# Attention times values on 128 partitions: one bank per pair of heads, copied behind the exponentials, and chunks of 55 columns

## The chip, the cores and the metric

The kernel runs on one core of a Trainium2 chip. The metric is the device time of one execution in microseconds (us); each time given is the median of three runs, and the profile is of one further execution.

## The reference

The reference is an attention with heads that are mixed before and after the softmax, followed by a gated feed-forward layer:

```python
batch, n_heads, seq, head_dim = (4, 12, 448, 64)          # B, H, S, D
scores = scale * np.matmul(q, k.transpose(0, 1, 3, 2))
scores = np.einsum('bhij,hg->bgij', scores, w_pre)
scores = scores - np.max(scores, axis=-1, keepdims=True)
attn = np.exp(scores)
attn = attn / (np.sum(attn, axis=-1, keepdims=True) + 1e-09)
attn = np.einsum('bhij,hg->bgij', attn, w_post)
x = np.matmul(attn, v)                    # then reshaped to 1792 x 768
xn = x / sqrt(mean(x * x) + 1e-06) * rms_g
out = (silu(xn @ w_gate) * (xn @ w_val)) @ w_out           # 768 -> 1536 -> 768
```

All inputs and outputs are float32.

## The kernel before

The program has two parts. Part A is the attention, up to about 360 us; part B is the feed-forward layer, and the change doesn't touch its code.

Part A cuts the 448 queries of each of the four batches into `NC` = 4 chunks of 120, 120, 120 and 100 columns (`OFF`, `PAIRS`), of which the last 12 are padding. A chunk is worked through in steps: `PAIRS` = 6, 6, 6, 5 steps, 92 in all (`T`). A step is called a pair (n, p): chunk n, pair p. Each step has two halves `u`, and each of them two groups `v_` of `RH` = 5 queries with all 12 heads, so that 60 rows of a 64-row tile are used.

The order of the instructions is written out by hand (`manual_schedule`, the loop over `t` at line 470). In step t TensorE issues, in this order:

- `premix` of step t (tile `sp`, line 186) in turn with `qk_mm` of a later chunk (tile `qk`, line 138). Both use tiles of 64 rows by 64 columns of the array.
- `postmix` of step t-1 (tile `pm`, line 227): 28 small products of 60 by 64, 60 columns each, which write the mixed attention transposed.
- `av_mm` (tile `av`, line 271): the product with v for a block of two chunks that are done, one half (`part` 0 or 1) of a pair of heads in each step. The stored attention `at_all` has keys on the partitions, in two halves `m` of 64; the two halves are multiplied by themselves in 64 by 64 tiles, and go to two PSUM banks `o[0]` and `o[1]`.

ScalarE (ACT) then does `av_copy` of both banks, if a pair of `av` was finished in the step before, and after it the exponentials `expo` (line 200), its half of the evacuation of `qk` (line 160, tile `st`) and its half of the evacuation of `pm` (line 242, `evac_a`). VectorE (DVE) takes the row maxima (line 193) and the other halves. GpSimd (POOL) adds the two copies of `av` (line 294, through `sum_ops`), squares and sums them (lines 301 to 309) and scales the weights of the next `postmix` (line 212, tile `wn`), which waits for the sums of the exponentials by way of VectorE (lines 207, 209). The sum of `av` is stored to memory on SyncE's queue (`x_store`), a step after POOL's addition.

The blocks are seven of two chunks (six pairs of heads in two parts each, so 84 parts) and the last two chunks alone (six whole pairs each). The 84 parts and the pairs of the last chunks stand in 83 steps, 13 to 95; the last four of them come after the last `premix`, among products of part B in float16 (lines 706 to 708, function `both`).

Of the kernel before, what the change touches and what calls it, by code (L numbers as in the profile page):

```python
# [7 lines left out]
F32 = mybir.dt.float32  # L8
# [3 lines left out]
AF = mybir.ActivationFunctionType  # L12
# [6 lines left out]
RH = 5  # L19
CHUNK = 120  # L20
NC = 4
PAIRS = [6, 6, 6, 5]
OFF = [0, 120, 240, 360]
SP_ = 460
HR = H * RH
GAP = H + 1
# [23 lines left out]
def attention_moe(ctx: ExitStack, tc, q, k, v, wpre, wpost, mask, ident, wgv, wo, rms_g, out):  # L50
# [64 lines left out]
        eng.dma_start(qt[n][:, hp], q[b, :, c, hp])  # L115

    def load_v(b, hp):
        t = vt[b, hp] = p1[0].tile([128, 2, JC, D], F32, name=f"v{b}_{hp}", tag=f"v{hp}")
        nc.sync.dma_start(t, v[b][:, 2 * hp : 2 * hp + 2])

    def halves_of(n, p):
# [7 lines left out]
    def banks(pl, name, many=2, at_=0):  # L129
        return [pl.tile([128, 512], F32, name=name, tag=f"{pl.name}{i}", bufs=1) for i in range(at_, at_ + many)]  # L130
# [19 lines left out]
    def qk_evac(n, hp, j):  # L150
        h, np_ = 2 * hp + j, PAIRS[n % NC]
        ps = qps[n, hp][j]
        if n == 0 and h < 1 or n == 1 and h < 2 * AHEAD:
            st = pro.tile([128, S], F32, name="st", tag="st", bufs=11)
        else:
            st = pq.tile([128, S], F32, name="st", tag="st", bufs=12)
        if j:
            nc.vector.tensor_copy(st, ps[:, :S])
        else:
            nc.scalar.activation(st, ps[:, :S], AF.Copy)  # L160
        for i, (lo, hi) in enumerate(((0, EARLY), (EARLY, 2 * np_)) if n == 0 else ((0, 2 * np_),)):
            w, at_ = RH * (hi - lo), 2 * RH * lo
            if h < H - 1:
                parts = [(h, 2 * RH, at_, 2 * w)]
            else:
                parts = [(h, RH, at_, w), (64, RH, at_ + w, w)]
            for row, k_, src, many in parts:
                dst = rt[n][row : row + (k_ - 1) * GAP + 1 : GAP, lo:hi]
                if i:
                    held.append((dst, st[src : src + many]))  # L170
                else:
                    turn = h if row < H else h + 1
                    if n:
                        eng = nc.gpsimd if n == 1 and 6 <= h < 2 * AHEAD else nc.sync
                    else:
                        eng = nc.sync if turn % 2 else nc.gpsimd if turn < 6 else nc.scalar
                    eng.dma_start(dst, st[src : src + many])

    def premix(n, p):
        ps = banks(ps_s, "sp", halves_of(n, p))  # L180
        sps[n, p] = ps

        def one(u, v_):
            sl = slice(64 * u, 64 * u + 64)
            o = ps[u][64 * v_ : 64 * v_ + 64, :S]
            nc.tensor.matmul(o, wk_pre[sl], rt[n][sl, 2 * p + v_], start=True, stop=True)  # L186

        return [[lambda u=u, v_=v_: one(u, v_) for v_ in range(2)] for u in range(len(ps))]

    def rowmax(n, p):  # L190
        for u, ps in enumerate(sps[n, p]):
# [22 lines left out]
    def postmix(n, p):  # L214
        ps = banks(ps_m, "pm")
        e, w = et.pop((n, p)), wn.pop((n, p))
        for u in range(2):
            u_ = min(u, len(e) - 1)
            for c in range(JC):
                for m in range(2) if c < JC - 1 else (u,):  # L220
                    j = min(2 * c + m, S // JT - 1) * JT
                    for v_ in range(2):
                        sl = slice(64 * v_, 64 * v_ + HR)
                        at_ = u * (JC - 1) + c if c < JC - 1 else JB - 1
                        o = ps[v_][64 * m : 64 * m + JT, : JB * HR].rearrange("p (s a i) -> p s a i", s=2, a=JB)
                        w_ = w[sl, u_].rearrange("p (s i) -> p s i", s=2)
                        nc.tensor.matmul(o[:, :, at_], e[u_][sl, j : j + JT], w_, start=True, stop=True)  # L227
        pm[n, p] = ps

    def evac_a(n, p, v_):  # L230
        if n == p == v_ == 0:
            pro_ctx.close()
            p2.append(pool(a_ctx, "p2", 2))
            p1.append(pool(a_ctx, "p1"))
        lo, hi = SLOTS[n]
        a = 2 * RH * p + RH * v_
        dst = at_all[:, lo : hi + 1 : hi - lo, :, a : a + RH]
        src = pm[n, p][v_][:, : JB * HR].rearrange("p (s x r) -> p s x r", s=2, r=RH)
        if v_:
            nc.vector.tensor_copy(dst, src)  # L240
        else:
            nc.scalar.activation(dst, src, AF.Copy)

    def heads_of(k):
        o = list(range(H // 2))
        return o[3:] + o[:3] if LATE_FIRST[k] else o

    def width(k):
        return sum(4 * RH * PAIRS[n % NC] for n in BLOCKS[k])

    def av_mm(k, at_, part):
        ns, hp = BLOCKS[k], heads_of(k)[at_]
        b, half = ns[0] // NC, 2 * hp // HH
        w = 2 * RH * PAIRS[ns[0] % NC]
        many = len(ns) * 2 * w
        if at_ % 2 == 0 and part != 1:
            xps[k, at_ // 2] = banks((ps_m, ps_v, ps_s)[at_ // 2] if ns[0] == NCHUNK - 1 else ps_v, "av")
        o = [x[:, (at_ % 2) * 240 : (at_ % 2) * 240 + many] for x in xps[k, at_ // 2]]
        sl_ = [SLOTS[n][half] for n in ns]
        a_ = at_all[:, sl_[0] : sl_[-1] + 1 : max(sl_[-1] - sl_[0], 1)].rearrange("p s (b h) i -> p s b h i", h=HH)  # L260
        for c_ in range(JC) if part is None else (2 * part, 2 * part + 1):
            for m in range(2):
                sl = slice(64 * m, 64 * m + JT)
                for j in range(2):
                    h = (2 * hp + j) % HH
                    x = o[m][64 * j : 64 * j + 64].rearrange("p (g u i) -> p g u i", u=2, i=w)
                    if c_ < JC - 1:
                        a = a_[sl, :, c_ : JB - 1 : JC - 1, h, :w]
                    else:
                        x, a = x[:, :, m], a_[sl, :, JB - 1, h, :w]  # L270
                    nc.tensor.matmul(x, vt[b, hp][sl, j, c_], a, start=(c_ == 0), stop=(c_ == JC - 1))  # L271

    def av_copy(k, i):
        ns = BLOCKS[k]
        w, full = [2 * RH * PAIRS[n % NC] for n in ns], 2 * 2 * RH * PAIRS[ns[0] % NC]
        xt[k, i] = [p2[0].tile([128, 2, width(k)], F32, name=f"xt{k_}", tag=f"xt{k_}", bufs=3) for k_ in range(2)]
        for t, x in zip(xt[k, i], xps.pop((k, i))):
            x = x[:, :480].rearrange("p (a i) -> p a i", i=240)
            if len(set(w)) == 1:
                nc.scalar.activation(t, x[:, :, : width(k)], AF.Copy)  # L280
            else:
                nc.scalar.activation(t[:, :, :full], x[:, :, :full], AF.Copy)
                rest = x[:, :, full:].rearrange("p a (u i) -> p a u i", u=2)[:, :, :, : w[1]]
                nc.scalar.activation(t[:, :, full:].rearrange("p a (u i) -> p a u i", u=2), rest, AF.Copy)

    ry, sq, sums, xv, d, scale_x = ({} for _ in range(6))
    sum_ops, stored = [], []

    def x_sum(k, i):
        b, c = divmod(BLOCKS[k][0], NC)  # L290
        x, t = xt[k, i]

        def add():
            nc.gpsimd.tensor_tensor(x, x, t, ALU.add)
            stored.append((k, i))

        if len(BLOCKS[k]) == 1:
            add()
        else:
            sum_ops.append(add)  # L300
# [9 lines left out]

    def x_store(k, i):
        b, c = divmod(BLOCKS[k][0], NC)
        x, hps = xt.pop((k, i))[0], heads_of(k)[2 * i : 2 * i + 2]
# [125 lines left out]
    def part_a(extra):  # L439
# [30 lines left out]
        for t in range(T + 24):  # L470
# [675 lines left out]
def layout(inputs):  # L1146
# [7 lines left out]
    qt = np.zeros((B, 2 * D, H // 2, SP_), np.float32)  # L1154
    qt[..., :S] = pairs(q)
    ql = np.zeros((B, 2 * D, NC, H // 2, 128), np.float32)
    for c, p in enumerate(PAIRS):
        u, r, t = np.meshgrid(np.arange(2), np.arange(RH), np.arange(2 * p), indexing="ij")
        i = np.minimum(OFF[c] + (u * 2 * p + t) * RH + r, SP_ - 1)
        ql[:, :, c, :, : 4 * RH * p] = qt[..., i.reshape(-1)]  # L1160
        if c == 0:
            i = np.concatenate([x.reshape(-1) for x in (i[..., :EARLY], i[..., EARLY:])])
            ql[0, :, c, :, : 4 * RH * p] = qt[0][..., i]
    kl = pairs(k)
    vl = np.zeros((B, H, JC * 128, D), np.float32)
    vl[:, :, :S] = v
    vl[:, :, S:] = v[:, :, S - JT :]
    vl = vl.reshape(B, H, JC, 128, D).transpose(0, 3, 1, 2, 4)

    def cols(w, kt):  # L1170
        w = np.ascontiguousarray(w)
# [45 lines left out]
```

## Time and profile before

| | |
|---|---|
| time, median of three runs | 830.21 us (828.98 to 832.03) |
| time of the profiled execution | 833.58 us |
| its span | 831.7 us |
| TensorE busy | 799.6 us, 10918 matmul instructions |
| VectorE busy | 633.1 us |
| ScalarE busy | 509.0 us |
| GpSimd busy | 354.1 us |

The span is the time from the first to the last instruction of the profiled execution; the 1.9 us between it and its time lie around the program. Busy times are of the engine alone; each float32 product stands as two matmul instructions and two weight loads. A matmul's end in the trace is modelled, so starts are what is compared below.

### The profile page before, as it was taken

The page shows a single profiled execution, that of the slowest core. Times are in us where ns is not written, and L with a number is a line of the kernel's source. Part 1 is how long each engine was busy: PE and PEld are TensorE (multiplying, and loading weights), DVE is VectorE, ACT ScalarE, POOL GpSimd, SP SyncE. Part 2 cuts the span into 40 slices and gives each one's busy share as a digit, 9 for nine tenths or more (in the row PEclk, how much of TensorE's full clock was granted, in tenths as well). Part 3 has the DMA queues.
Part 4 walks back from the last instruction along what each step waited for, and adds up shares of the span by engine and source line. Part 5 has one row for each costly group of instructions (what it writes and reads, how often), then busy time and mean ns, then how long its engine had stood idle before and what let it go on. Part 6 is the DMA issues. An engine that isn't in the chain of part 4 may idle for free.

```text
span 831.7 us, 27130 instructions
## 1 busy us (share of the span) xinstructions
PE 799.6 (96%) x10918; PEld 488.9 (59%) x10918; DVE 633.1 (76%) x1318; ACT 509.0 (61%) x1129; POOL 354.1 (43%) x467
## 2 busy tenths in 40 slices
PE   7899987999989999899999999999999999999998
PEld 2567766877767767655555555555555555555555
DVE  5777877797878877789589978997889776547562
ACT  3676767677767775774444554455445555969850
POOL 7212343353435435771533532525344358462310
PEclk9999999999999999999999999999999999999999
DMA  7778778667886665373446544753656345566641
GB/s 209 200 218 222 221 231 233 194 192 209 223 237 181 202 202 155 105 240 122 138 140 189 140 146 111 214 183 106 180 147 198 101 154 178 137 208 177 180 142 67
DMA packets 82383, 146.15 MB, mean 176 GB/s; under 512 B 10527, under 2 KB 73277, under 8 KB 82259
## 3 DMA queue, kind: packets, MB, share of 16 engines
q1 hardware_dynamic: 80462, 140.81, 56.5%
q0 software_dynamic: 832, 2.06, 1.0%
q8 instruction: 86, 1.41, 0.7%
q10 hardware_dynamic: 965, 1.56, 0.6%
q14 instruction: 38, 0.31, 0.1%
HBM read 72.83 MB, written 32.00 MB: 126 GB/s over the span
## 4 chain that ended last, share of the span: by engine, by line
PE 91%; issue 3%; DMA 3%; DVE 2%; ACT 1%; POOL 0%; ACTq 0%; SPq 0%; POOLq 0%; DVEq 0%
PE pm L227 9%; PE av L271 8%; PE qk L138 8%; PE sp L186 8%; PE pg L715 6%; PE pv L717 6%; PE pv L715 6%; PE pg L717 6%; PE pv L716 6%; PE pg L716 6%; PE po L717 6%; PE po L716 6%; PE po L715 6%; DMA r<-st 2%; DMA q<-in_q 1%
## 5 line engine op out<-in xcount | busy, mean ns | idle before, releaser
L200 ACT ACTIVATE e<-sp,nm 128x448 f32<-128x448 f32 x180 | 114.3, 638 | 90.8 <-DVE nm L193 88.7
L186 PE MATMUL sp<-r,wk_pre 64*64 64x448 f32 x720 | 163.9, 541 | 1.6 <-ACT e L200 1.0
L138 PE MATMUL qk<-k,q 64*64 64x448 f32 x768 | 153.6, 559 | 7.5 <-DMA q<-in_q 4.5
L193 DVE TENSOR_REDUCE nm<-sp 128x1 f32<-128x448 f32 x180 | 110.5, 620 | 42.1 <-PE sp L186 18.5
L212 POOL TENSOR_SCALAR wn<-wk,rp 128x60 f32<-128x60 f32 x180 | 60.8, 352 | 190.7 <-DVE rp L209 129.2
L227 PEld LDWEIGHTS pm<-wn,e 60*64 60x64 f32 x5152 | 110.3, 134 | 50.0 <-POOL wn L212 22.2
L227 PE MATMUL pm<-wn,e 60*64 60x60 f32 x5152 | 111.3, 220 | 15.2 <-issue 12.6
L763 POOL TENSOR_TENSOR sg<-sg,u 128x448 f32<-128x448 f32 x36 | 46.7, 1297 | 150.4 <-ACT sg L760 103.0
L271 PE MATMUL av<-at_all,v 64*64 64x240 f32 (+4 forms) x1728 | 95.9, 322 | 3.8 <-issue 3.7
L716 PE MATMUL pv<-x,wh 128*128 128x448 f16 x264 | 93.0, 352 | 0.0
L717 PE MATMUL pv<-x,wl 128*128 128x448 f16 x264 | 93.0, 352 | 0.0
L715 PE MATMUL pg<-x,wh 128*128 128x448 f16 x264 | 93.0, 352 | 0.0
L715 PE MATMUL pv<-x,wh 128*128 128x448 f16 x264 | 93.0, 352 | 0.0
L716 PE MATMUL pg<-x,wh 128*128 128x448 f16 x264 | 93.0, 352 | 0.0
L717 PE MATMUL pg<-x,wl 128*128 128x448 f16 x264 | 93.0, 352 | 0.0
L717 PE MATMUL po<-h,fac 128*128 128x448 f16 (+1 forms) x258 | 89.8, 348 | 0.0
L715 PE MATMUL po<-h,fac 128*128 128x448 f16 (+1 forms) x258 | 89.8, 348 | 0.0
L716 PE MATMUL po<-h,fac 128*128 128x448 f16 (+1 forms) x258 | 89.8, 348 | 0.0
L715 PEld LDWEIGHTS <-wh 128*128 128x128 f16 x528 | 51.7, 98 | 48.2 <-issue 0.2
L716 PEld LDWEIGHTS <-wh 128*128 128x128 f16 x528 | 51.7, 98 | 48.3 <-issue 0.3
L717 PEld LDWEIGHTS <-wl 128*128 128x128 f16 x528 | 51.7, 98 | 48.2
L271 PEld LDWEIGHTS av<-at_all,v 64*64 64x64 f32 x1728 | 71.3, 134 | 7.5 <-issue 6.8
(167 smaller groups left out, 1564.4 us busy)
## 6 DMA issues: line engine op xcount, KB each, us to landing
r<-st SPq DMA_DIRECT2D x117, 210.0 KB
hraw<-td SPq DMA_DIRECT2D x84, 224.0 KB
wraw<-in_wgv SPq DMA_DIRECT2D x20, 768.0 KB
td<-keep SPq DMA_DIRECT2D x48, 224.0 KB
wraw<-in_wo SPq DMA_DIRECT2D x12, 768.0 KB
r<-st SPq DMA_DIRECT2D x44, 175.0 KB
v<-in_v SPq DMA_DIRECT2D x24, 256.0 KB
k<-in_k SPq DMA_DIRECT2D x24, 224.0 KB
```

Source lines behind the costliest of these rows:

```text
L138: nc.tensor.matmul(ps[j][m, :S], qt[n][sl, hp, m], kt[n // NC, hp][sl], start=True, stop=True)
L186: nc.tensor.matmul(o, wk_pre[sl], rt[n][sl, 2 * p + v_], start=True, stop=True)
L193: nc.vector.tensor_reduce(t, ps[:, :S], AX.X, ALU.max, negate=True)
L200: nc.scalar.activation(e, ps[:, :S], AF.Exp, bias=nmx.pop((n, p, u)), accum_out=sm[n, p][:, u : u + 1])
L212: nc.gpsimd.tensor_scalar(wn[n, p][:, u], wk, r[:, u : u + 1], 1.0, ALU.mult, ALU.mult)
L227: nc.tensor.matmul(o[:, :, at_], e[u_][sl, j : j + JT], w_, start=True, stop=True)
L271: nc.tensor.matmul(x, vt[b, hp][sl, j, c_], a, start=(c_ == 0), stop=(c_ == JC - 1))
L715: nc.tensor.matmul(ps, a, xh[:, kk, at_], start=(kk == 0), stop=False)
L716: nc.tensor.matmul(ps, a, xl_[:, kk, at_], start=False, stop=False)
L717: nc.tensor.matmul(ps, a2, xh[:, kk, at_], start=False, stop=(kk == KT - 1))
L763: nc.gpsimd.tensor_tensor(h, sg, u, ALU.mult)
```

## The change

The product with v takes all 128 partitions at once: a weight tile is 128 rows by 64 columns, and the two heads of a pair stand in two column tiles. The last 64 keys, which the two halves of a chunk hold on different partitions, are multiplied with v padded with zeros above or below (`JC + 1` = 5 blocks of v). The two partial sums thus meet in one PSUM bank, which alternates from pair to pair. `av_copy` copies one bank instead of two and stands behind the exponentials; POOL's addition is gone. The third and fourth chunk are 55 and 50 columns wide in each half (`WIDE`): the twelfth group of the third chunk belongs to the fourth. The last step of a fourth chunk then has one `postmix` of 14 products instead of 28, and its evacuation is in two instructions on each engine.

```diff
-OFF = [0, 120, 240, 360]
+OFF = [0, 120, 240, 350]
+WIDE = [60, 60, 55, 50]
+GROUPS = [12, 12, 12, 9]
...
     def av_mm(k, at_, part):
...
-        w = 2 * RH * PAIRS[ns[0] % NC]
+        w = WIDE[ns[0] % NC]
         many = len(ns) * 2 * w
         if at_ % 2 == 0 and part != 1:
-            xps[k, at_ // 2] = banks((ps_m, ps_v, ps_s)[at_ // 2] if ns[0] == NCHUNK - 1 else ps_v, "av")
+            last = ns[0] == NCHUNK - 1
+            xps[k, at_ // 2], = banks((ps_m, ps_v, ps_s)[at_ // 2] if last else ps_v, "av", 1, 0 if last else len(pairs_done) % 2)
+            pairs_done.append(k)
...
-        for c_ in range(JC) if part is None else (2 * part, 2 * part + 1):
-            for m in range(2):
-                sl = slice(64 * m, 64 * m + JT)
-                for j in range(2):
-                    h = (2 * hp + j) % HH
-                    x = o[m][64 * j : 64 * j + 64].rearrange("p (g u i) -> p g u i", u=2, i=w)
-                    if c_ < JC - 1:
-                        a = a_[sl, :, c_ : JB - 1 : JC - 1, h, :w]
-                    else:
-                        x, a = x[:, :, m], a_[sl, :, JB - 1, h, :w]
-                    nc.tensor.matmul(x, vt[b, hp][sl, j, c_], a, start=(c_ == 0), stop=(c_ == JC - 1))
+        for c_ in range(JC + 1) if part is None else ((0, 1), (2, 3, 4))[part]:
+            for j in range(2):
+                h = (2 * hp + j) % HH
+                o = x[64 * j : 64 * j + 64].rearrange("p (g u i) -> p g u i", u=2, i=w)
+                if c_ < JC - 1:
+                    a = a_[:, :, c_ : JB - 1 : JC - 1, h, :w]
+                else:
+                    o, a = o[:, :, c_ - JC + 1], a_[:, :, JB - 1, h, :w]
+                nc.tensor.matmul(o, vt[b, hp][:, j, c_], a, start=(c_ == 0), stop=(c_ == JC))
...
     def x_sum(k, i):
...
-        def add():
-            nc.gpsimd.tensor_tensor(x, x, t, ALU.add)
-            stored.append((k, i))
...
-            for a in done:
-                av_copy(*a)
             if back(0):
                 rowmax(*back(0))
                 expo(*back(0))
+            for a in done:
+                av_copy(*a)
```

TensorE's instructions around the first two parts of a pair of heads, before (pair of heads 4 of the first block; its part 0 and then its part 1):

```order
L227 MATMUL pm<-wn,e 64x2x30 x28
L271 MATMUL av<-at_all,v_4_757 64x240 x8
L186 MATMUL sp<-r_123,wk_pre 64x448 x2
L138 MATMUL qk<-k_2_965,q_825 64x448 x2
L186 MATMUL sp<-r_123,wk_pre 64x448 x2
L138 MATMUL qk<-k_2_965,q_825 64x448 x2
L227 MATMUL pm<-wn,e 64x2x30 x28
L271 MATMUL av<-at_all,v_4_757 64x240 x4
L271 MATMUL av<-at_all,v_4_757 64x2x60 x4
```

The same place of the changed kernel:

```order
L226 MATMUL pm<-wn,e 64x2x30 x28
L296 MATMUL av<-at_all,v_4_757 64x240 x4
L187 MATMUL sp<-r_123,wk_pre 64x448 x2
L140 MATMUL qk<-k_2_965,q_825 64x448 x2
L187 MATMUL sp<-r_123,wk_pre 64x448 x2
L140 MATMUL qk<-k_2_965,q_825 64x448 x2
L226 MATMUL pm<-wn,e 64x2x30 x28
L296 MATMUL av<-at_all,v_4_757 64x240 x2
L296 MATMUL av<-at_all,v_4_757 64x2x60 x4
```

The places are the same; part 0 has four products where eight stood, in two column tiles side by side instead of four tiles, and part 1 has six where eight stood.

ScalarE's instructions around the first copy of `av`, before:

```order
L160 ACTIVATE st<-qk 128x448
L242 ACTIVATE at_all<-pm 128x2x42x5
L280 ACTIVATE xt_1425<-av 128x480
L280 ACTIVATE xt_1426<-av 128x480
L200 ACTIVATE e,s<-sp,nm 128x448 x2
L160 ACTIVATE st<-qk 128x448
L242 ACTIVATE at_all<-pm 128x2x42x5
```

And in the changed kernel:

```order
L162 ACTIVATE st<-qk 128x448
L265 ACTIVATE at_all<-pm 128x2x42x5
L203 ACTIVATE e,s<-sp,nm 128x448 x2
L305 ACTIVATE xt<-av 128x480
L162 ACTIVATE st<-qk 128x448
L265 ACTIVATE at_all<-pm 128x2x42x5
```

One copy is left of two; it moved from ahead of the two exponentials to behind them, ahead of that step's evacuations of `qk` and `pm`.

## Rows read from the trace of the kernel before

**Rows 1.** The page: busy time of each engine, share of the span, instructions.
```profile
PE 799.6 (96%) x10918; PEld 488.9 (59%) x10918; DVE 633.1 (76%) x1318; ACT 509.0 (61%) x1129; POOL 354.1 (43%) x467
```

**Rows 2.** Busy time by stretch: PE, PEld, DVE, ACT, POOL, granted clock, DMA.
```profile
100.00:150.00 50.00, 42.96 (x1120) 33.38 (x1116) 34.90 (x87) 33.87 (x93) 18.36 (x38) 0.97 0.78 229
...
450.00:500.00 50.00, 50.00 (x267) 25.84 (x265) 42.35 (x77) 25.29 (x47) 20.64 (x15) 1.00 0.50 152
```

**Rows 3.** The chain of work, steps around 171 to 194: start, duration, what.
```profile
170.87 0.82 PE pm L227 x45
171.69 0.67 PE av L271 x16
...
173.86 0.77 PE pm L227 x41
...
174.68 0.82 PE av L271 x15
...
176.99 0.77 PE pm L227 x40
...
179.94 0.81 PE pm L227 x50
183.11 0.82 PE pm L227 x44
186.51 0.91 PE pm L227 x40
```

**Rows 4.** The chain among the last products with v, 353 to 359.
```profile
353.78 1.41 PE av L271 x64
355.19 0.30 PE pg L706
...
355.87 0.19 PE pv L706
...
356.43 1.41 PE av L271 x64
```

**Rows 5.** The chain of 75 to 340: its first and last step, and a wait.
```profile
75.17 0.80 PE pm L227 x49
...
142.15 3.15 issue
...
335.04 1.08 PE pm L227 x47
```

**Rows 6.** Who waited for whom, 50 to 345: total us, times, longest.
```profile
ACT e L200 <- DVE nm L193: 76.2, 79, 3.5
...
PEld pm L227 <- POOL wn L212: 19.0, 51, 1.4
...
PE pm L227 <- issue: 11.4, 14, 3.1
...
PE av L271 <- issue: 3.7, 5, 1.2
```

**Rows 7.** The page: the DMA queue that carries instructions.
```profile
q8 instruction: 86, 1.41, 0.7%
```

**Rows 8.** ScalarE in order of time, 172 to 174.
```profile
172.22 0.53 ACT L160 ACTIVATE st<-qk 128x448 f32<-128x448 f32 x1
172.64 0.62 ACT L242 ACTIVATE at_all<-pm 128x420 f32<-128x420 f32 x1
173.10 1.04 ACT L280 ACTIVATE xt<-av 128x480 f32<-128x480 f32 x2
173.99 0.68 ACT L200 ACTIVATE e<-sp,nm 128x448 f32<-128x448 f32 x1
```

**Rows 9.** GpSimd's groups, 50 to 345: busy, mean ns, idle before and its releasers.
```profile
L212 POOL TENSOR_SCALAR wn<-wk,rp 128x60 f32<-128x60 f32 x161 | 55.0, 356 | 166.8 <-DVE rp L209 105.3 <-PE sp L186 20.0 <-DVE square L602 7.6
L294 POOL TENSOR_TENSOR xt<-xt,xt 128x480 f32<-128x480 f32 (+2 forms) x22 | 25.3, 1150 | 0.0
```

**Rows 10.** Weight loads of 128 rows in part B, whole run: busy, mean ns.
```profile
L715 PEld LDWEIGHTS <-wh 128*128 128x128 f16 x528 | 51.7, 98 | 48.2 <-issue 0.2
```

More of the change, by code (lines that the diff above doesn't have):

```diff
@@ L117, in load_v @@
     def load_v(b, hp):
-        t = vt[b, hp] = p1[0].tile([128, 2, JC, D], F32, name=f"v{b}_{hp}", tag=f"v{hp}")
+        t = vt[b, hp] = p1[0].tile([128, 2, JC + 1, D], F32, name=f"v{b}_{hp}", tag=f"v{hp}")
         nc.sync.dma_start(t, v[b][:, 2 * hp : 2 * hp + 2])
@@ L160, in qk_evac @@
             nc.scalar.activation(st, ps[:, :S], AF.Copy)
-        for i, (lo, hi) in enumerate(((0, EARLY), (EARLY, 2 * np_)) if n == 0 else ((0, 2 * np_),)):
+        for i, (lo, hi) in enumerate(((0, EARLY), (EARLY, 2 * np_)) if n == 0 else ((0, GROUPS[n % NC]),)):
             w, at_ = RH * (hi - lo), 2 * RH * lo
@@ L181, in premix, with one @@
         sps[n, p] = ps
-        def one(u, v_):
+        def one(u, v_, o):
             sl = slice(64 * u, 64 * u + 64)
-            o = ps[u][64 * v_ : 64 * v_ + 64, :S]
             nc.tensor.matmul(o, wk_pre[sl], rt[n][sl, 2 * p + v_], start=True, stop=True)
-        return [[lambda u=u, v_=v_: one(u, v_) for v_ in range(2)] for u in range(len(ps))]
+        if len(ps) == 1:
+            return [[lambda u=u: one(u, 0, ps[0][64 * u : 64 * u + 64, :S])] for u in range(2)]
+        return [[lambda u=u, v_=v_: one(u, v_, ps[u][64 * v_ : 64 * v_ + 64, :S]) for v_ in range(2)] for u in range(2)]
     def rowmax(n, p):
@@ L216, in postmix, with one @@
         e, w = et.pop((n, p)), wn.pop((n, p))
-        for u in range(2):
-            u_ = min(u, len(e) - 1)
-            for c in range(JC):
[L220 to L227, printed above, removed]
+        def one(bank, rows, u, c, m, e_, w_):
+            j = min(2 * c + m, S // JT - 1) * JT
+            sl = slice(64 * rows, 64 * rows + HR)
+            at_ = u * (JC - 1) + c if c < JC - 1 else JB - 1
+            o = bank[64 * m : 64 * m + JT, : JB * HR].rearrange("p (s a i) -> p s a i", s=2, a=JB)
+            nc.tensor.matmul(o[:, :, at_], e_[sl, j : j + JT], w_[sl].rearrange("p (s i) -> p s i", s=2), start=True, stop=True)
+        if len(e) == 1:
+            for c in range(JC):
+                for m in range(2) if c < JC - 1 else (0,):
+                    for u in range(2):
+                        one(ps[u], u, u, c, m if c < JC - 1 else u, e[0], w[:, 0])
+        else:
+            for u in range(2):
+                for c in range(JC):
+                    for m in range(2) if c < JC - 1 else (u,):
+                        for v_ in range(2):
+                            one(ps[v_], v_, u, c, m, e[u], w[:, u])
         pm[n, p] = ps
@@ L234, in evac_a @@
             p1.append(pool(a_ctx, "p1"))
-        lo, hi = SLOTS[n]
-        a = 2 * RH * p + RH * v_
+        c, t = n % NC, 2 * p + v_
+        if c == 2 and t == 11:
+            n_, a = n + 1, 40
+        elif c < NC - 1:
+            n_, a = n, RH * t
+        else:
+            n_, a = n, 45 if p == PAIRS[-1] - 1 else RH * t
+        lo, hi = SLOTS[n_]
         dst = at_all[:, lo : hi + 1 : hi - lo, :, a : a + RH]
         src = pm[n, p][v_][:, : JB * HR].rearrange("p (s x r) -> p s x r", s=2, r=RH)
-        if v_:
-            nc.vector.tensor_copy(dst, src)
-        else:
-            nc.scalar.activation(dst, src, AF.Copy)
+        if halves_of(n, p) == 1:
+            n3 = (JC - 1) * HH
+            parts = [(slice(0, 128), slice(n3 * v_, n3 * v_ + n3)), (slice(64 * v_, 64 * v_ + 64), slice(2 * n3, JB * HH))]
+        else:
+            parts = [(slice(0, 128), slice(0, JB * HH))]
+        for rows, x in parts:
+            if v_:
+                nc.vector.tensor_copy(dst[rows, :, x], src[rows, :, x])
+            else:
+                nc.scalar.activation(dst[rows, :, x], src[rows, :, x], AF.Copy)
     def heads_of(k):
@@ L248, in width @@
     def width(k):
-        return sum(4 * RH * PAIRS[n % NC] for n in BLOCKS[k])
+        return sum(2 * WIDE[n % NC] for n in BLOCKS[k])
+    pairs_done = []
     def av_mm(k, at_, part):
@@ L253, in av_mm @@
         b, half = ns[0] // NC, 2 * hp // HH
-        w = 2 * RH * PAIRS[ns[0] % NC]
+        w = WIDE[ns[0] % NC]
         many = len(ns) * 2 * w
         if at_ % 2 == 0 and part != 1:
-            xps[k, at_ // 2] = banks((ps_m, ps_v, ps_s)[at_ // 2] if ns[0] == NCHUNK - 1 else ps_v, "av")
-        o = [x[:, (at_ % 2) * 240 : (at_ % 2) * 240 + many] for x in xps[k, at_ // 2]]
+            last = ns[0] == NCHUNK - 1
+            xps[k, at_ // 2], = banks((ps_m, ps_v, ps_s)[at_ // 2] if last else ps_v, "av", 1, 0 if last else len(pairs_done) % 2)
+            pairs_done.append(k)
@@ L259, in av_mm @@
+        x = xps[k, at_ // 2][:, (at_ % 2) * 240 : (at_ % 2) * 240 + many]
         sl_ = [SLOTS[n][half] for n in ns]
         a_ = at_all[:, sl_[0] : sl_[-1] + 1 : max(sl_[-1] - sl_[0], 1)].rearrange("p s (b h) i -> p s b h i", h=HH)
[L261 to L271 removed]
+        for c_ in range(JC + 1) if part is None else ((0, 1), (2, 3, 4))[part]:
[4 more added lines that the diff above has]
+                    a = a_[:, :, c_ : JB - 1 : JC - 1, h, :w]
+                else:
+                    o, a = o[:, :, c_ - JC + 1], a_[:, :, JB - 1, h, :w]
+                nc.tensor.matmul(o, vt[b, hp][:, j, c_], a, start=(c_ == 0), stop=(c_ == JC))
@@ L273, in av_copy @@
     def av_copy(k, i):
         ns = BLOCKS[k]
[L275 to L284, printed above, removed]
+        w = [WIDE[n % NC] for n in ns]
@@ new lines, in av_copy @@
+        full = 2 * w[0]
+        t = xt[k, i] = p2[0].tile([128, 2, width(k)], F32, name="xt", tag="xt", bufs=3)
+        x = xps.pop((k, i))[:, :480].rearrange("p (a i) -> p a i", i=240)
+        if len(set(w)) == 1:
+            nc.scalar.activation(t, x[:, :, : width(k)], AF.Copy)
+        else:
+            nc.scalar.activation(t[:, :, :full], x[:, :, :full], AF.Copy)
+            more = x[:, :, full : 2 * full].rearrange("p a (u i) -> p a u i", u=2)[:, :, :, : w[1]]
+            nc.scalar.activation(t[:, :, full:].rearrange("p a (u i) -> p a u i", u=2), more, AF.Copy)
@@ L286, in attention_moe @@
+        stored.append((k, i))
     ry, sq, sums, xv, d, scale_x = ({} for _ in range(6))
@@ L290, in x_sum @@
         b, c = divmod(BLOCKS[k][0], NC)
-        x, t = xt[k, i]
-        def add():
-            nc.gpsimd.tensor_tensor(x, x, t, ALU.add)
-            stored.append((k, i))
[L297 to L300, printed above, removed]
+        x = xt[k, i]
+        t = p2[0].tile([128, 2, width(k)], F32, name="xq", tag="xq", bufs=1)
         sum_ops.append(lambda: nc.gpsimd.tensor_tensor(t, x, x, ALU.mult))
@@ L312, in x_store @@
         b, c = divmod(BLOCKS[k][0], NC)
-        x, hps = xt.pop((k, i))[0], heads_of(k)[2 * i : 2 * i + 2]
+        x, hps = xt.pop((k, i)), heads_of(k)[2 * i : 2 * i + 2]
         cols = slice(OFF[c], OFF[c] + width(k))
@@ L1152, in pairs @@
         return x.reshape(B, H // 2, 2, S, D).transpose(0, 2, 4, 1, 3).reshape(B, 2 * D, H // 2, S)
-    qt = np.zeros((B, 2 * D, H // 2, SP_), np.float32)
-    qt[..., :S] = pairs(q)
+    qt = pairs(q)
     ql = np.zeros((B, 2 * D, NC, H // 2, 128), np.float32)
[L1157 to L1160, printed above, removed]
+    for c in range(NC):
+        u, r, t = np.meshgrid(np.arange(2), np.arange(RH), np.arange(GROUPS[c]), indexing="ij")
+        i = OFF[c] + WIDE[c] * u + RH * t + r
+        if c == 2:
+            i = np.where(t == 11, OFF[3] + WIDE[3] * u + 40 + r, i)
+        if c == 3:
+            i = np.minimum(np.where(t == 8, i + RH, i), S - 1)
+        ql[:, :, c, :, : i.size] = qt[..., i.reshape(-1)]
         if c == 0:
             i = np.concatenate([x.reshape(-1) for x in (i[..., :EARLY], i[..., EARLY:])])
-            ql[0, :, c, :, : 4 * RH * p] = qt[0][..., i]
+            ql[0, :, c, :, : i.size] = qt[0][..., i]
     kl = pairs(k)
-    vl = np.zeros((B, H, JC * 128, D), np.float32)
+    vl = np.zeros((B, H, (JC + 1) * 128, D), np.float32)
     vl[:, :, :S] = v
-    vl[:, :, S:] = v[:, :, S - JT :]
-    vl = vl.reshape(B, H, JC, 128, D).transpose(0, 3, 1, 2, 4)
+    vl[:, :, -JT:] = v[:, :, S - JT :]
+    vl = vl.reshape(B, H, JC + 1, 128, D).transpose(0, 3, 1, 2, 4)
     def cols(w, kt):
```

## The prediction

> **What bounds the kernel now.** I read the busy times first, then the stretches, then the chain. TensorE is busy for 96% of the span [rows 1], but the stretches show two regimes: in part B it is never idle (50.00 of 50 us), in part A it idles 7 us of 50 at worst, with the granted clock at 0.97 there and at full speed elsewhere [rows 2]. Only part A is touched, so the question is what a step of part A costs.
>
> The chain answers it. Three steps in a row start their `postmix` at 170.87, 173.86 and 176.99 [rows 3]: 2.99 us for a step with part 1 of the product with v, 3.13 us for one with part 0. All of it is TensorE at work: 0.82 us of `pm`, 0.67 or 0.82 us of `av`, and the rest `sp` with `qk`. I call these clean steps. Others are longer, as 183.11 to 186.51 (3.40 us) in the same group. From 75.17 to 335.04 the chain has 72 steps in 259.9 us [rows 5]. 32 clean steps of each kind make 195.8 us, and the eight steps with both parts at most 8 x (2.99 + 0.82) = 30.5 us; so TensorE waits some 34 us in these steps, about 0.48 us in each, and very unevenly. Set beside the clean length of its kind, step by step through the `pm` rows of the chain (first and last are [rows 5]), 26 of the 72 steps wait under 0.15 us (1.3 us in sum), 19 wait 0.15 to 0.5 us (5.6 us), 27 wait longer (29 us).
>
> What is waited for differs: weights `wn` from POOL, 19.0 us in 51 short waits, and waits without a releaser in the middle of `pm` and `av`, 11.4 + 3.7 us [rows 6], the longest 3.15 us [rows 5]. I take these for instruction fetch: one queue brings 86 packets in 1.41 MB [rows 7], and TensorE's 2 x 10918 instructions [rows 1] are 254 a packet. That is an inference; no row names it.
>
> **The change, part by part.** *Streaming.* Two quads of four 64 by 64 tiles with 240 columns take 0.82 us [rows 3], so a quad takes 0.41 us. A pair of heads has 3.5 quads now (0.5 for the last 64 keys): 1.44 us. Afterwards it has five pairs of column tiles, three with all columns and two with half: 4 x 0.41 = 1.64 us if the two column tiles run side by side as the four tiles do. For the four blocks of 240 columns that is +0.205 us for each of 24 pairs of heads, 4.9 us. The three blocks with the third chunk have 220 columns: 4 x 0.376 = 1.50 us, +0.07 us for 18, 1.2 us. The last two chunks alone add 6 x (0.75 - 0.72) and 6 x (0.68 - 0.60), 0.7 us. Sum: **+6.8 us**.
>
> *Switching the array.* Everything in part A is now in tiles of 64 by 64; afterwards `av` has 128 rows, between `pm` and `sp`, in each of 83 steps. What such a switch costs stands at the end of part A, where `av` alternates with float16 products on the whole array [rows 4]. The 64 instructions of two pairs of heads with 100 columns should take 2 x 3.5 x 0.41 x 100/240 = 1.20 us and take 1.41 (353.78 to 355.19): +0.21. The six float16 products should take 6 x 0.19 = 1.14 us and take 1.24 (355.19 to 356.43): +0.10. A round trip costs 0.31 us. Four of the 83 steps already pay it; 79 are new: 79 x 0.31 = **+24.5 us**. From below, the bound is nothing: no row has a switch from 64 by 64 to 128 by 64. I take the whole 0.31, since rows 4 are the nearest case and 128 rows are common to both.
> The Trainium skill (TensorEngine Tiling (Array Packing), Key Properties) says that changing the tiling mode, unlike changing the tile, drains the engine; by that sentence the sum would be the same 24.5 us. The trace agrees for the whole array (0.31 us a round trip) and doesn't show the mode of 128 by 64.
>
> *Fewer products elsewhere.* `postmix` halves in four steps: 4 x 0.41 = **-1.6 us**. All in all TensorE gets +29.7 us of work.
>
> *What of it lies under waits.* A wait for `wn`, for exponentials or for an evacuation runs from the `sp` of a step, and the added work lies between that `sp` and the waiting instruction: it shortens the wait by as much as it lengthens the work. So a step grows by what exceeds its wait. A step with part 0 gets 0.31 us (0.24 with 220 columns), one with part 1 gets 0.52 (0.45). The 26 nearly clean steps pay 8.1 us, the 19 middle ones 3.3, the 27 long ones nothing: **+11.4 us**, and 0.5 us more at the end, where the chain is TensorE alone [rows 4].
>
> *Instructions.* Part A issues 2 x 760 = 1520 fewer TensorE instructions of 16736 (648 products with v and 112 of `postmix`, each with its load): 9%. The 15.1 us of waits without a releaser [rows 6] should lose that share, and, if they are fetches, more: a packet of 254 lasts some 1.4 steps and so gains 1.4 x 0.4 us of slack, of which the count by steps has 0.4. With ten waits that matter: **-3.5 us** (bounds 0 and -10).
>
> *ScalarE.* 27 copies of 0.52 us (1.04 us for two [rows 8]) are gone and the others move behind the exponentials. Before, the copies ran from 173.10 to 173.99, when the exponential came [rows 8]; they filled a gap, since ScalarE waits 76.2 us for the row maxima anyway [rows 6]. So no gain there. Behind the copy now queue that step's copy `st` and `evac_a`, for which the next `pm` waits. `evac_a` ends at 173.26 [rows 8] and the next `pm` begins at 173.86 [rows 3]: 0.60 us of room for 0.52 us. Cover just holds, and added TensorE work widens it; cost nothing. `x_store` on SyncE's queue now waits for that copy, which is ahead of the `st` copies that the queue waits for next: nothing.
>
> *POOL.* 27 additions of 1.15 us go; POOL waits 166.8 us before its `wn`, mostly for VectorE's reciprocal [rows 9]. No gain, and at the very end a store that starts about 1 us earlier under part B's products.
>
> *Sum.* +11.4 + 0.5 - 1.6 - 3.5 = +6.8 us on the profiled 833.58 (span 831.7, 1.9 around it). That execution is 3.4 us above the median, so the same step on the median gives 830.2 + 6.8 = **837.0 us**, 0.8% slower. Half a per cent, 4.2 us, is about what a measurement of this kernel can tell from no change.
>
> **The rivals.**
> *No switch is paid between 64 by 64 and 128 by 64* (faster). Then TensorE gets 6.8 - 1.6 = 5.2 us, nearly all in steps with part 1, +0.2 or +0.13 us each; under the waits about 1 us stays. With -1.6 and -3.5 that makes -4 us: 826, bounds 822 and 830. For it: the column tiles stay as they are, 64 wide. Against it: rows 4. It decides where a round trip costs under about 0.1 us.
> *The waits take nearly everything* (no change). If the waits without a releaser shrink to their bound of -10 us instead of -3.5, the sum is about 0: 830, bounds 826 to 834. For it: 27 of 72 steps wait more than is added. Against it: 26 wait for nothing.
> *The copy delays `evac_a`* (slower). If the room of 0.60 us isn't there in steps that are late already, 27 steps lose up to 0.5 us each: +7 to +13 on the forecast, 847. Against it: the step gets longer too.
> *Weight loads of 128 rows are not hidden* (slower). Each `pm` tile takes a load and a product every 0.82/14 = 0.06 us, so a load of 64 columns costs at most that; ten in a row for each of 54 pairs of heads, exposed, are 32 us more: 865. Against it: in part B loads of 98 ns [rows 10] lie under products of 0.19 us apart [rows 4].
> The Trainium skill (TensorE: Matmul & The Clock Gate, Part 3: Packing small matmuls) says that a load overlaps running products only when the row group differs, which would make this rival true; rows 10 with rows 4 speak against it for the whole array.
>
> **How the numbers follow.** Forecast (slower by 4 to 12 us) 0.48; no switch paid 0.18, of which 0.13 faster and 0.05 within half a per cent; waits take it 0.26; late `evac_a` 0.05; loads exposed 0.03. Slower by over 0.5%: 0.56; within: 0.31; faster: 0.13. The forecast's own range is 834 to 843. The range of 8 in 10 leaves out the loads, the worse half of the late `evac_a` and the better half of the first rival: 824 to 846.
>
> **What would show it.** Steps of 3.4 to 3.5 us for both parts, with fewer over 4 us; the first `av` about 0.1 us after the end of `pm`, and the first `sp` about as late after `av`; `av` at 0.82 us in both parts; fewer and shorter waits without a releaser; POOL's line of additions gone and ScalarE's exponentials at unchanged places in the step. I am wrong if `av` follows `pm` without a gap, or if the long waits go altogether.

## The result and the profile after

The changed kernel takes 837.13 us (median of 12 runs, 834.61 to 840.31), the kernel before 832.07 us beside it (12 runs, 827.58 to 835.27). The ratio is 1.0067, with a 95% interval from 1.0042 to 1.0091: 5.6 us slower (3.5 to 7.6), where +6.8 us were predicted. (The predicted 837.0 us stood on the median of three runs, which was 1.9 us below that of the 12.) The profiled execution took 837.89 us (span 836.1), 4.4 us more in the span than the one shown of before. Ratios, here and below, leave out executions more than 1.5% above the fastest of the same kernel: three of the 12 in experiment 1, at 831.6 to 834.1 us, and none elsewhere.

The page of the changed kernel, busy time of each engine:

```profile
PE 818.1 (98%) x10158; PEld 466.8 (56%) x10158; DVE 632.7 (76%) x1322; ACT 499.0 (60%) x1097; POOL 321.1 (38%) x440
```

Against [rows 1] TensorE issues 760 matmul instructions fewer and is busy 18.5 us longer; its idle time fell from 32.1 us of the span to 18.0. ScalarE and POOL have less to do by 10 and 33 us, for which nothing was booked. The stretches (busy time of PE, PEld, DVE, ACT, POOL, then the granted clock):

```profile
100.00:150.00 50.00, 50.00 (x1159) 31.54 (x1154) 40.01 (x100) 35.62 (x97) 16.69 (x39) 1.00 0.80 230
...
300.00:350.00 50.00, 48.46 (x1070) 32.48 (x1064) 35.51 (x102) 30.55 (x79) 20.77 (x52) 0.97 0.49 147
```

The stretch that was the worst in [rows 2], 100 to 150, has no idle time of TensorE left, and the granted clock is 1.00 in it. What is missing from 300 to 350, and the clock of 0.97 there, come nearly all from one place at 343 (below). So the work was added, and the waits went. The chain of work around 172 shows the step (start, duration, what):

```profile
172.24 0.86 PE pm L226 x52
173.10 0.96 PE av L296 x8
174.06 0.52 PE sp L187 x2
...
175.73 0.86 PE pm L226 x48
176.59 0.97 PE av L296 x12
177.56 0.52 PE sp L187
...
179.22 0.86 PE pm L226 x42
```

Both kinds of step now last 3.49 us (172.24 to 175.73 with part 0, 175.73 to 179.22 with part 1). Against the 3.13 and 2.99 us of [rows 3] that is +0.36 and +0.50 us; +0.31 and +0.52 were predicted. What became longer is read from the same rows: `av` takes 0.96 us where its columns take 0.82 (+0.14), from its end to the next `pm` 1.67 us pass where 1.50 did (+0.17), together the 0.31 us of a round trip; part 1 now has 0.82 us of columns too, as part 0 does, and `pm` is longer by 0.04. By start times, in the step at 172.24, the first `av` comes 0.15 us after the last `pm`, where one `pm` follows the other in its tile after 0.06, and the first `sp` 0.30 us after the last `av`, where one `av` follows the other after 0.20: about 0.1 us at either place, as forecast. Who waited for whom, 50 to 345 (total us, times, longest):

```profile
ACT e L203 <- DVE nm L196: 90.6, 84, 3.4
...
PEld pm L226 <- POOL wn L215: 18.3, 66, 0.8
...
PE pm L226 <- issue: 2.7, 3, 1.6
```

The waits without a releaser fell from 11.4 + 3.7 us [rows 6] to 2.7, and those for `wn` are shorter (0.8 us at most instead of 1.4) though more in number. The exponentials wait longer for the row maxima (90.6 us instead of 76.2), so ScalarE has no less time to spare than before. Of the 72 steps that [rows 5] bound, 12 are longer than 4 us instead of 15, and six of the 12 are so because they have both parts. In the chain from 74 to 340, waits without a releaser of over 0.2 us stood 16 times between TensorE's own instructions before (15.3 us); one is left (1.61 us, at 243.84).

### The profile page after: what moved, and what is told of

It reads as the page before. It is cut to its first block, busy times and chain, and to the rows that moved or that the text cites. A ratio compares the mean times of both kernels' runs of the same rounds, so it can differ in the third digit from the quotient of the medians.

```text
span 836.1 us, 25480 instructions
## 1 busy us (share of the span) xinstructions
PE 818.1 (98%) x10158; PEld 466.8 (56%) x10158; DVE 632.7 (76%) x1322; ACT 499.0 (60%) x1097; POOL 321.1 (38%) x440
## 4 chain that ended last, share of the span: by engine, by line
PE 93%; DMA 2%; DVE 1%; ACT 1%; issue 1%; ACTq 0%; SPq 0%; DVEq 0%
PE sp L187 10%; PE av L296 9%; PE pm L226 9%; PE qk L140 8%; PE pg L733 6%; PE pv L735 6%; PE pv L733 6%; PE pg L735 6%; PE pg L734 6%; PE pv L734 6%; PE po L735 6%; PE po L734 6%; PE po L733 6%; DMA r<-st 2%; PE pg L724 1%
## 5 line engine op out<-in xcount | busy, mean ns | idle before, releaser
L140 PE MATMUL qk<-k,q 64*64 64x448 f32 x768 | 155.8, 567 | 5.9 <-DMA q<-in_q 4.1
L187 PE MATMUL sp<-r,wk_pre 64*64 64x448 f32 x720 | 157.2, 549 | 3.9 <-ACT e L203 2.1
L226 PEld LDWEIGHTS pm<-wn,e 60*64 60x64 f32 x5040 | 100.7, 134 | 43.4 <-POOL wn L215 20.0
L226 PE MATMUL pm<-wn,e 60*64 60x60 f32 x5040 | 100.9, 220 | 4.0 <-issue 3.8
L296 PE MATMUL av<-at_all,v 128*64 128x240 f32 (+6 forms) x1080 | 93.4, 310 | 0.0
L716 DVE TENSOR_TENSOR h<-hps,h 128x448 f16<-128x448 f32 x72 | 44.0, 621 | 33.7 <-ACT h L715 33.7
```

The costliest lines, as they stand in the source:

```text
L140: nc.tensor.matmul(ps[j][m, :S], qt[n][sl, hp, m], kt[n // NC, hp][sl], start=True, stop=True)
L226: nc.tensor.matmul(o[:, :, at_], e_[sl, j : j + JT], w_[sl].rearrange("p (s i) -> p s i", s=2), start=True, stop=True)
L296: nc.tensor.matmul(o, vt[b, hp][:, j, c_], a, start=(c_ == 0), stop=(c_ == JC))
L716: nc.vector.tensor_tensor(lo, t, hi, ALU.subtract)
```

## The experiments

All ratios are to the kernel before, timed on the same chip beside each: 829.03 us (29 runs) for experiments 1, 3, 5 and 7, 831.11 us (18 runs) for 2, 4, 6 and 8.

**1. The widths alone.** The kernel before with the new `OFF`, `WIDE` and `GROUPS`, the halved `postmix` and its evacuation; the product with v stays in two halves and two banks.

```diff
-OFF = [0, 120, 240, 360]
+OFF = [0, 120, 240, 350]
+WIDE = [60, 60, 55, 50]
+GROUPS = [12, 12, 12, 9]
```

> The kernel before with one part of the change alone: the widths of 55 and 50, the groups, the single postmix of 14 products and the evacuation that belong to them. The product with v stays in tiles of 64 by 64, in two banks, copied ahead of the exponentials and added by POOL. Theory A (the switch of the array between 64 by 64 and 128 by 64 is what costs): without the switch the time is below that of before, by up to 1.6 us of postmix and 2 us of narrower products, part of it under waits: 828 to 831 against 832, ratio 0.995 to 1.0. Rival B (the widths, with their evacuation in two instructions, cost the time): 835 to 838, ratio 1.004 to 1.008.

Measured: 826.14 us (12 runs), ratio 0.9932 (0.9893 to 0.9970), 5.6 us faster. That is a little better than was expected; but the ratio rests on nine of the 12 runs, and by the medians of all of them (826.14 against 829.03 us, 0.9965) the gain is 2.9 us. I take it as 3 to 6 us. This beats both kernels. The halved `postmix` (-1.6 us) and 3.5 quads shorter by 20 of 240 columns in 18 pairs of heads (18 x 3.5 x 0.41 x 20/240 = 2.2 us) make 3.8 us, which lies within it.

**2. The product on 128 rows alone.** The kernel before with the padded v, one bank and the copy behind the exponentials, but with the old chunks.

```diff
+        for c_ in range(JC + 1) if part is None else ((0, 1), (2, 3, 4))[part]:
...
+                    a = a_[:, :, c_ : JB - 1 : JC - 1, h, :w]
+                else:
+                    o, a = o[:, :, c_ - JC + 1], a_[:, :, JB - 1, h, :w]
```

> The kernel before with the other part of the change alone: the product with v on 128 rows in one bank that alternates, copied once behind the exponentials; widths, groups and postmix as before. Theory A (the two parts add up: widths alone gave 0.993, all gave 1.007): ratio 1.010 to 1.017. Rival (the widths gain only where waits are left, so that under 128 rows they gave nothing): ratio 1.005 to 1.009.

Measured: 840.66 us (6 runs), ratio 1.0127 (1.0084 to 1.0170), 10.6 us slower. The two halves of the change add up, as far as the intervals tell: 0.9932 x 1.0127 = 1.0058 (1.009 with the medians of experiment 1), beside 1.0067 for both. The whole loss is the product's, and the widths hide a third to a half of it.

**3. One more switch in the changed kernel.** A product of 128 rows and one column ahead of `postmix` in the 80 steps that have `av`, so that the array goes from 64 by 64 to 128 by 64 and back once more. Its result lies in a column that nothing reads.

```diff
+        if trip[0]:
+            nc.tensor.matmul(ps[0][:64, 500:501], ones[:, :64], ones[:, :1], start=True, stop=True)
```

> The changed kernel, with the same extra product at the same places: a second round trip in each of 80 steps. Theory A (round trip 0.31 us plus a second weight load of about 0.06, and the steps of the changed kernel have hardly any waits left to cover it): +24 to +30 us on 837, so 861 to 867, ratio to before 1.035 to 1.042. Rival B (the switch is free): at most +8 us, ratio under 1.017. Rival C (the changed kernel still has as many waits as before): +8 to +14 us, ratio 1.016 to 1.024.

**4. The same product without a switch.** As 3, but 64 rows by 64 columns, the tile of its neighbours.

```diff
-            nc.tensor.matmul(ps[0][:64, 500:501], ones[:, :64], ones[:, :1], start=True, stop=True)
+            nc.tensor.matmul(ps[0][:64, 500:501], ones[:64, :64], ones[:64, :1], start=True, stop=True)
```

> The changed kernel with the tiny extra product of e3_switch_after made 64 by 64, the mode that the array is in at that place: the same place, bank and waits, no switch. Theory A (a switch costs, the tiny product hardly anything): at most +5 us on the changed kernel, ratio to before 1.004 to 1.013. Rival (the product itself, with its wait for the bank and its two loads, made the 22 us of e3_switch_after): ratio 1.025 or more.

Measured: with the switch 858.72 us (6 runs), ratio 1.0345 (1.0304 to 1.0386); without it 840.69 us (7 runs), ratio 1.0101 (1.0065 to 1.0137). Against the changed kernel's 1.0067 these are +23 and +3 us. The chains show what a step has of it, with the switch (`pm` on line 222 is the added product):

```profile
174.53 0.21 PE pm L222 x2
174.73 1.01 PE pm L230 x46
175.75 0.96 PE av L300 x8
176.71 0.52 PE sp L187 x2
...
178.38 0.21 PE pm L222 x2
```

and without:

```profile
176.46 0.99 PE pm L230 x49
177.45 0.96 PE av L300 x8
178.41 0.52 PE sp L187 x2
...
180.06 0.99 PE pm L230 x50
```

A step lasts 3.85 us with the switch (174.53 to 178.38) and 3.60 us without (176.46 to 180.06): 0.25 us is the round trip, 0.11 us over the 3.49 us of the changed kernel the product itself. In the time, (23 - 3) / 80 = 0.25 us again (0.20 to 0.31 by the intervals). So nothing hides the switch here. The product itself is hidden in part: 80 x 0.11 = 9 us by the chain, 3 us in the time (-1 to 6). The changed kernel still had short waits for `wn`, 18.3 us of them; with the added product in each step there are hardly any left to give, as the waits of this run from 50 to 345 show:

```profile
PEld pm L230 <- POOL wn L215: 1.4, 5, 0.3
```

The rival by which nothing is paid between these two modes falls. The two added products differ in the rows of their weights too, 128 and 64, so a longer load that isn't hidden would count as part of the 0.25 us.

**5. The same switch in the kernel before.** The edit of 3, on the kernel before.

> The kernel before, with one tiny extra product of 128 by 64 (one column, into a spare column of postmix's bank) ahead of postmix in each of the 80 steps that have both a postmix and a product with v: one round trip of the array's mode more for each, and nothing else. Theory A (a round trip costs 0.31 us and the waits of before cover most of it): steps that are clean grow by 0.3 to 0.45 us, the sum is +4 to +14 us on 832, ratio 1.005 to 1.017. Rival B (64 by 64 to 128 by 64 is free): only the product itself, at most 0.12 us a step and mostly under waits: ratio 0.999 to 1.004.

Measured: 833.56 us (12 runs), ratio 1.0047 (1.0022 to 1.0072): 3.9 us, where the changed kernel lost 23. The work was added here too. The chain shows steps of 3.55 us (172.43 to 175.98; it was 3.13) with the added product ahead of `pm` (0.21 us), `pm` itself 0.2 us longer and the rest of the step as it was:

```profile
172.43 0.21 PE pm L219 x2
172.64 1.01 PE pm L231 x50
173.65 0.82 PE av L275 x16
174.47 0.31 PE sp L186
...
175.98 0.21 PE pm L219 x2
```

But the waits gave way. Its page:

```profile
PE 818.8 (98%) x11078; PEld 479.3 (58%) x11078; DVE 639.5 (77%) x1318; ACT 511.0 (61%) x1129; POOL 352.9 (42%) x467
...
q8 instruction: 87, 1.43, 0.7%
```

and its waits, 50 to 345:

```profile
PEld pm L231 <- POOL wn L212: 1.2, 4, 0.3
...
PE av L275 <- issue: 1.1, 1, 1.1
...
PE pm L231 <- issue: 0.3, 1, 0.3
```

TensorE has 160 more instructions than in [rows 1] and the queue of [rows 7] has one packet more, and yet the waits without a releaser are 1.4 us instead of 15.1, those for `wn` 1.2 instead of 19.0. So they don't go with the number of instructions, as the prediction had it. That they go with the pace, since a step that lasts 0.4 us longer leaves whatever they wait for that much more time, fits all eight profiles whose steps are longer than before (3.6 us or less in `pm` and `av` together), but it isn't the whole of it: experiment 1, at the pace of before, has half of the 15.1 us, and each kernel was profiled once.

```profile
PE pm L226 <- issue: 5.8, 6, 1.6
...
PE av L294 <- issue: 1.0, 2, 0.9
```

**6. Fewer round trips.** The changed kernel with both parts of a pair of heads in one step and none in the next, with otherwise the same instructions. The trace has 50 stretches of `av` instead of 83, so 33 round trips fewer.

```diff
-            t = lo + i * (hi - lo) // len(units)
+            t = lo + (i | 1 if a[2] is not None else i) * (hi - lo) // len(units)
```

> The changed kernel with both parts of a pair of heads in one step, every second step having none: some 36 round trips of the array's mode fewer, the same products. Theory A1 (the step is TensorE's work alone): 36 x 0.3 = -11 us on the changed kernel, ratio to before 0.992 to 0.998. Theory A2 (a step without a product with v is held at about 3.0 us by the chain from sp over rowmax, exponential and wn to postmix, as in the first steps of the kernel before, and the step with both is TensorE's 4.3 us): two steps take 7.3 us instead of 6.9, +14 us, ratio 1.018 to 1.028.

Measured: 853.62 us (6 runs), ratio 1.0256 (1.0217 to 1.0295), 16 us slower than the changed kernel. The chain of two steps, among blocks of 220 columns:

```profile
219.98 0.86 PE pm L226 x52
220.84 0.89 PE sp L187 x4
...
223.05 1.03 PE pm L226 x46
224.08 1.64 PE av L296 x20
225.72 0.52 PE sp L187 x2
...
227.39 0.86 PE pm L226 x54
```

Both parts together take 1.64 us, that is two times 0.75 and one drain of 0.14, so a drain is saved. But the step without `av`, which has 0.86 + 1.50 = 2.4 us of work, lasts 3.07 us (219.98 to 223.05). The weight loads of that step say what holds it (idle time ahead and its releaser in brackets):

```profile
221.73 0.17 PEld L187 LDWEIGHTS sp<-r,wk_pre 64*64 64x64 f32 x2 [0.21 <-ACT e L203]
...
222.99 0.44 PEld L226 LDWEIGHTS pm<-wn,e 60*64 60x64 f32 x24 [0.72 <-POOL wn L215]
```

`premix` waits for the exponentials, and `postmix` for `wn`, which come through VectorE and POOL. Such a step takes about 3.0 us, however little TensorE has to do in it; the steps ahead of the first product with v, which have none either, take 3.06 us in both kernels (60.15 to 63.21 before, 62.20 to 65.26 after, by the starts of `pm`). I take it that this is also what the steps of before met: at 2.99 and 3.13 us they ran just at the pace of that chain, and a delay became a wait.

**7. The copy ahead of the exponentials.** The changed kernel with `av_copy` where it stood before.

```diff
+            for a in done:
+                av_copy(*a)
             if back(0):
                 rowmax(*back(0))
                 expo(*back(0))
-            for a in done:
-                av_copy(*a)
```

> The changed kernel with the one copy of the product with v ahead of the exponentials again, as before. Theory A (the copy's place is hidden either way): the same as the changed kernel within 2 us, ratio to before 1.004 to 1.009. Rival D (behind the exponentials the copy holds up the evacuation of postmix, and that is part of the loss): faster than the changed kernel by 3 us or more, ratio under 1.003. Rival E (the place behind the exponentials is worth something, since ahead of them the copy delays them): slower by 3 us or more, ratio over 1.010.

Measured: 833.71 us (12 runs), ratio 1.0056 (1.0027 to 1.0085), not to be told from 1.0067. ScalarE of the changed kernel in order of time, where [rows 8] stood for before:

```profile
173.63 0.56 ACT L305 ACTIVATE xt<-av 128x480 f32<-128x480 f32 x1
...
174.51 0.55 ACT L265 ACTIVATE at_all<-pm 128x420 f32<-128x420 f32 x1
175.73 0.64 ACT L203 ACTIVATE e<-sp,nm 128x448 f32<-128x448 f32 x1 [0.68 <-DVE nm L196]
```

and with the copy ahead:

```profile
172.22 0.57 ACT L305 ACTIVATE xt<-av 128x480 f32<-128x480 f32 x1
173.50 0.64 ACT L203 ACTIVATE e<-sp,nm 128x448 f32<-128x448 f32 x1 [0.71 <-DVE nm L196]
```

Behind the exponentials the copy delays `evac_a` to 175.06, still 0.67 us ahead of the `pm` at 175.73; ahead of them it runs where ScalarE waits for the row maxima anyway, and leaves 0.71 us of that wait. Either place is free, to within the 3 us that the intervals leave.

**8. Without the second padded product.** The changed kernel without the last of the five blocks of v, so that the last 64 keys of the second half are left out of the product.

```diff
-        for c_ in range(JC + 1) if part is None else ((0, 1), (2, 3, 4))[part]:
+        for c_ in range(JC) if part is None else ((0, 1), (2, 3))[part]:
```

> The changed kernel without the second of the two zero-padded products of a pair of heads; it leaves out the last 64 keys of the second half of each chunk. Theory A (the changed kernel is bound by TensorE in nearly every step, so streamed columns cost what they stream): 24 pairs of heads by 0.205 us, 18 by 0.188 and 12 by 0.09, 9.4 us less than the changed kernel, less what waits give back: -5 to -9.4 us, ratio to before 0.995 to 1.001. Rival (the extra streaming lies under waits, only the switch shows): -2 us or less, ratio 1.003 to 1.008.

Measured: 832.84 us (12 runs), ratio 1.0016 (0.9988 to 1.0044), some 4 us less than the changed kernel, from some 9 us of columns (24 pairs of heads at 0.205 us, 18 at 0.19 and the last chunks). That is just short of the 5 to 9.4 us expected, and more than the rival's 2. The profile doesn't show steps that wait more for it: from the first `av` to the last `sp` it takes 275.6 us (66.64 to 342.19) where the changed kernel takes 283.4 (66.39 to 349.80), 8 us less, and the waits for `wn` are 19.5 us instead of 18.3. But this execution is 3.0 us below the median of its 12. The mean granted clock over the 12 runs is 0.9965, where it is 0.9987 for the changed kernel; an estimate from that, 0.0022 of 833 us, makes 1.8 us. What took the rest in the other runs is open.

## Why the prediction came out, step by step

*The step.* Its two terms, streaming and the switch, are right in size, and so is the mechanism: +0.36 and +0.50 us a step in the profile, +0.31 and +0.52 predicted. The round trip, taken as 0.31 us from a neighbouring case, is 0.14 + 0.17 = 0.31 us in the step and 0.25 us where it was measured alone (experiments 3 and 4). The Trainium skill (TensorEngine Tiling (Array Packing), Key Properties) says that a change of the tiling mode drains the engine; the trace now agrees for 64 by 64 to 128 by 64 as well, with these 0.25 to 0.31 us. It also shows what the switch takes away. From 66 to 345 us the first weight load of `av` starts before the last `pm` in 76 of 79 steps before, and in none of 77 after; the first load of `sp` or `qk` starts before the last `av` in 69 of 80 steps before, and in none of 77 after. Work that ran ahead under its neighbour between tiles of one mode no longer does across the change.

*Weight loads* of 128 rows are hidden but for the first two: there are 8 of them, at 136 ns each, for the 0.96 us of a part 0. The first two, one for each column tile, start with the first products (173.03), behind `pm`, and may be part of the 0.14 us above; the others start under products. Loads from 50 to 345 (busy us, mean ns, idle before):

```profile
L296 PEld LDWEIGHTS av<-at_all,v 128*64 128x64 f32 x900 | 52.4, 136 | 14.7
```

and the products of the same stretch:

```profile
L296 PE MATMUL av<-at_all,v 128*64 128x240 f32 (+4 forms) x900 | 85.2, 324 | 0.0
```

*What the waits take.* Here the sum was wrong, though the total came out. The prediction let 26 clean steps pay in full and gave 3.5 us back for fewer instructions, +6.3 us with the halved `postmix` for the middle of part A. In the two profiles the 72 steps from 75.17 to 335.04 [rows 5], 259.9 us, became 259.1: 0.8 us less, though 32 x 0.36 + 32 x 0.50 + 8 x 0.86 = 34 us of work were added in them, less some 3 for narrower blocks and halved `postmix`. Clean steps did pay, but the waits of the others went nearly altogether, which the prediction had named as what would speak against it. The reason given for the 3.5 us, fewer instructions to fetch, fell with experiment 5; what the waits without a releaser wait for is still not shown. One thing more wasn't booked: the mean granted clock is 0.997 and 0.996 over the runs of before timed beside the experiments, and 0.9987 over the 12 of the changed kernel. An estimate from that: 0.0017 to 0.0026 of 830 us, 1.4 to 2.2 us, came back by the clock. Whether it goes with the waits is open: experiments 3 to 5, with hardly any waits, have 0.999, but experiment 8, with few, has 0.9965.

*What the tail took.* The 72 steps begin 1.7 us later than before (76.88 instead of 75.17), for which nothing was booked and whose cause is open. The prediction booked 0.5 us behind the last steps; between the two profiles it is 3.3 us (from the `pm` that starts at 338.18 before and at 339.32 after to the first product of part B's own loops, 46.9 us and 50.2). Two things make up most of it. First the instructions around 340 to 343, in order of time:

```profile
340.19 1.49 DVE L828 SCALAR_TENSOR_TENSOR wl<-wf,stats,wh 128x384 f16<-128x384 f32 x1
340.29 0.98 POOL L319 TENSOR_TENSOR xq<-xt 128x480 f32<-128x480 f32 x1
...
343.10 1.63 PE L187 MATMUL sp<-r,wk_pre 64*64 64x448 f32 x8 [1.38 <-ACT e L203]
```

VectorE's conversion of a weight stands ahead of the row maxima and takes 1.49 us beside a POOL instruction (0.61 us in the profile of experiment 7), so that the exponentials come late and TensorE is idle for 1.38 us. Then the granted clock falls (columns as in the stretches above):

```profile
342.00:344.00 2.00, 0.90 (x6) 0.39 (x8) 1.46 (x5) 1.68 (x6) 0.24 (x1) 1.00 0.22 74
344.00:346.00 2.00, 2.00 (x10) 0.59 (x5) 1.28 (x3) 1.37 (x3) 0.60 (x2) 0.63 0.40 82
346.00:348.00 2.00, 2.00 (x41) 1.15 (x43) 1.16 (x3) 1.28 (x4) 0.00 (x0) 0.52 0.66 203
```

The 0.52 is nearly the lower level, 1.2 GHz instead of 2.4, and the products take twice as long, as the chain shows:

```profile
345.21 0.37 PE pg L725
...
347.08 1.42 PE pm L226 x54
...
352.44 0.19 PE pg L725
```

Idle 1.38 us, six float16 products that take 2.36 us instead of 1.24 (344.72 to 347.08; 352.15 to 353.39 at full speed), and a `pm` of 1.42 instead of 0.86 us: 3.1 us. The long conversion stands in the profiles of the changed kernel and of experiments 2, 3, 4, 6 and 8, all with the copy behind the exponentials; with the copy ahead of them (before, experiments 1, 5 and 7) it takes 0.61 to 0.67 us. So it goes with the copy's place, but its price doesn't show in the ratio of experiment 7. The clock fell behind it in two profiles alone, this one and that of experiment 8; in the other four with the long conversion it stayed at 1.00. That part differs from one execution to the next.

The last products with v came as the terms had it: two pairs of heads with 100 columns, 2 x 4 x 0.41 x 100/240 = 1.37 us, with 0.21 us for the switch 1.58, take 1.63 us (357.54 in the chain).

*The rest.* Of the rivals, that no switch is paid, that the copy delays `evac_a` and that weight loads are exposed fell with experiments 4, 7 and the rows above; that the waits take nearly everything came true for the middle of part A, not for the time. Nothing was booked for ScalarE and POOL; experiment 7 agrees for the place of the copy, and no run puts POOL's addition back. The widths were booked with 1.6 us and the shorter columns inside the streaming term; alone they are worth 3 to 6 us, which doesn't exclude the 3.8 us worked out above. The product alone then costs 10.6 us (7.0 to 14.1), where the same terms make at least 6.8 + 1.6 = 8.4.

So the time was met with errors of opposite sign within the sum: a middle that lost nothing between these two profiles instead of 6.3 us, and a start and a tail that lost 1.7 and 2.8 us more than was booked. That they nearly cancel is luck. The mechanism around them is what the experiments confirm: work of TensorE is added in each step, and the waits, once used up, take no more.

## What to carry to other kernels

Price a reordering of TensorE's work in a step by the step's own clean length, and then ask how much wait the step has left to cover it: the same 80 added products with their switches cost 4 us in a kernel with waits and 23 us in one with hardly any left. Keep neighbouring products in one tiling mode where the step is bound by TensorE; here a mode of 128 rows saved POOL 33 us that nobody waited for and cost TensorE 0.31 us in every step. Time the parts of a bundled change apart: half of this one is a gain of 0.3 to 0.7%, the other a loss of 1.3%.

## What was not expected of the hardware

Waits of TensorE without a releaser, 15.1 us in the kernel before, nearly vanish (1.4 us) when each step has 0.4 us more work and the program has more instructions, not fewer; half of them are gone in experiment 1 too (6.8 us), for which the pace gives no reason. Across a change from tiles of 64 by 64 to 128 by 64 neither a weight load nor a product starts ahead of the last product of the other mode (0 of 77 steps, 76 of 79 for the loads of `av` without the change). A step without the product with v took 3.07 us for 2.4 us of TensorE's work, since exponentials, `wn` and `postmix` of successive steps make a chain of their own. And one idle time of 1.4 us at the end of part A was followed by some 4 us at a granted clock of 0.63 and 0.52, which cost 1.7 us, more than the idle time did; in the profile of experiment 2 TensorE was idle for 2.9 us between 340 and 360, and the clock stayed at 1.00.
